# Every batch's ninth chunk moved to the last four tiles, and router weights and row fills issued one at a time between the loads

## The chip, the core and the metric

The kernel runs on one core of one Trainium2 chip. The metric is the device time of one execution in microseconds (us); lower is better. The times below are the median of three executions, and the profile is of one further execution of the same program.

## What is computed

Attention inside chunks of 64 tokens, then a two-level mixture of experts on the result, all in float32:

```python
B, H, S, D = 8, 8, 576, 64                 # 9 chunks of 64 tokens in each batch
scores = (q_c @ k_c.T) / 8                 # within one chunk of 64, per head
out = softmax(scores) @ v_c
x = out.transpose(0, 2, 1, 3).reshape(4608, 512)   # one row per token
g_idx = argmax(x @ w_group)                # 4 groups
e_idx = argmax(x @ w_expert[g_idx])        # 4 experts in each group
h = relu(x @ w1[g, e])                     # 512 -> 1024
y = combined_weight * (h @ w2[g, e])       # 1024 -> 512, written to the token's row
```

Each token goes to one of 16 experts. The order in which tokens are worked on is free, as long as each result lands in its own row.

## The kernel before

**Tiles.** The 72 chunks are numbered c = 0..71 and two neighbours make a tile of 128 tokens, so there are 36 tiles. Before, chunk c is chunk c % 9 of batch c // 9. `load_qk(n)`, written Qn, brings q and k of four chunks (two tiles) into one buffer, two tokens in a partition, so that four chunks fill 128 partitions and one chunk fills 32. `load_v(t)`, written Vt, brings v of one tile, 64 partitions for a chunk. Both ask `spans(c0, n)` into which pieces a run of chunks falls, and issue one DMA for each piece; a piece ends where a batch ends. The q and k buffers are three in rotation, those of v eight. All these DMAs are issued by SyncE (SP) on one queue, one behind the other.

**The loop.** Iteration t of the first stage (t = 0..26; then a hand-written string, TAIL) issues for TensorE: the scores of tile t (`stage_b`, line 308), P times V of tile t-2 (`stage_pv`, line 344), two `stage_a` steps that transpose raw q and k of tiles further on (line 286; step a(4n) is the first to read load Qn), the transpose of the probabilities (331) and of x (373). After every fourth tile a group of 512 tokens is routed: `stage_e1` multiplies x by the router weights `wg` (line 380), first in iteration 7; `stage_e3` and `place` compute each token's row in its expert's region of the DRAM buffer `xs`, and GpSimd (POOL) writes the rows there by four indirect DMAs (line 514). The order of TensorE, VectorE and ScalarE is the program's own; that of SP and POOL is made by a scheduler from the program's order and what each step waits for.

**What else SP issues.** After the two steps of an iteration come the load Q(t/2+4) in even iterations, V(t+4), and what `EXTRA[t]` lists: `Z0`..`Z4` (`prefill`) fill five blocks of 128 rows of `xs` from the tile `pad`, and `G0` (`load_wg`) brings the router weights, five DMAs in a row, and makes two small copies on VectorE and one on GpSimd. The indirect writes to `xs` wait until all five fills have landed.

**The second stage** works expert by expert on the rows of `xs`, from line 738 on. How many units it has, and of which kinds, follows from how many tokens each expert has in all; the expert that goes first is the one with most tokens after four groups.

Of the kernel before, what the change touches and what calls it, by code (L numbers as in the profile page):

```python
# [19 lines left out]
P = 128  # L20
B, H, SEQ, HD = 8, 8, 576, 64
CH = 64
NCH = SEQ // CH
N = B * SEQ
D = H * HD
F = 1024
G, EG = 4, 4
E = G * EG
NT = N // P
NG = 4  # L30
RPE = N // P
GL = NT // NG - 1
# [10 lines left out]

HEAD = "Q0 @ Q1 V0 Q2 V1 V2 V3 a0 a1"
FIRST = "a2 a3 Q3 a4 a5 a6"
EXTRA = {0: "Z0 Z1", 1: "G0 Z2", 2: "Z3", 3: "Z4",
         24: "F0", 26: "F1"}
T0 = 27
TAIL = ("m2 a60 b27 E0 p25 V31 s27 15 l5 n25 c26 m1 P0 a61 e27 j0 x24 25 b28 F2 m1 F3 s28 P1 a62 c27 p26 m1 e28 a63 V32"
# [8 lines left out]
C_ID, C_TRI, C_SEL, C_BASE, C_IOTA4, C_TID, C_T17, C_I64, C_J128, C_FORCE, C_BE, C_PBASE, C_E, C_PM, C_I16, C_PJ, C_PQ, C_PMIN, C_PNEED, C_N = (  # L58
    0, 128, 256, 276, 292, 296, 332, 349, 413, 449, 450, 451, 452, 453, 455, 471, 473, 475, 476, 477)
# [4 lines left out]
BIG = 1 << 20  # L64


def constants():
    c = np.zeros((P, C_N), np.float32)
    p = np.arange(P)
    c[:, C_ID:C_ID + P] = np.eye(P)  # L70
    c[:, C_TRI:C_TRI + P] = p[:, None] < p[None, :]
    for j in range(20):
        c[p % 32 == j, C_SEL + j] = 1.0
    for j, rows in enumerate((32, RE - 32)):
        c[j, C_BASE:C_BASE + E] = np.arange(E) * rows * P
    c[:, C_IOTA4:C_IOTA4 + 4] = np.arange(4)
    c[:, C_TID:C_TID + NT] = np.arange(NT)[None, :] * P + p[:, None]

    o = np.roll(np.arange(E1), -1)
    c[:E1, C_T17:C_T17 + E1] = o[:, None] < o[None, :]  # L80
    c[:E1, C_I64:C_I64 + 64] = np.arange(64)
    c[:E1, C_J128:C_J128 + RPE] = np.arange(RPE) * P
    c[:E1, C_FORCE] = o < FORCED
    c[:E, C_BE] = (np.arange(E) * RE - E * RE) * P
    c[:E, C_PBASE] = np.arange(E) * RE * P
    c[0, C_PMIN] = c[0, C_PNEED] = 2 * P
    c[1:FORCED - 1, C_PNEED] = P
    c[:E1, C_E] = np.arange(E1)
    c[0, C_PM], c[0, C_PM + 1] = 1.0, -1.0
    c[:, C_I16:C_I16 + E] = np.arange(E) - 64.0  # L90
    for j in range(2):
        c[0, C_PJ + j] = j * P + P - 1
        c[0, C_PQ + j] = j * P + 64 * RE * P - E * RE * P
    return c


def moe_kernel(tc, q, k, v, w_group, w_expert, w1, w2, cst, out):
    nc = tc.nc
    w1 = w1.rearrange("g e d f -> (g e) d f")
    w2 = w2.rearrange("g e f d -> (g e) f d")  # L100
    with ExitStack() as ctx:
# [12 lines left out]
        nc.gpsimd.memset(pad, 0.0)  # L114
        nc.gpsimd.memset(pad[:, D:D + 1].bitcast(I32), N)

# [94 lines left out]
        with ExitStack() as c1:  # L211
# [15 lines left out]
            wg = cpool.tile([P, 4, 32], F32, name="wg")  # L227
# [9 lines left out]
            def spans(c0, n):  # L237
                out, c = [], c0
                while c < c0 + n:
                    b, j = divmod(c, NCH)  # L240
                    m = min(c0 + n - c, NCH - j)
                    out.append((c - c0, m, b, j))
                    c += m
                return out

            def load_qk(n):

                if n == 0:
                    raw = lpool.tile([P, 2, 2, H, HD], F32, name="qk", tag="big")
                    parts = [(1, t, raw[:, t], slice(None)) for t in range(2)]  # L250
                else:
                    raw = lpool.tile([P, 2, H, 2 * HD], F32, name="qk", tag="big")
                    parts = [(2, 2 * n, raw, slice(None))]
                st["q", n] = raw
                for A, t0, dst, hs in parts:
                    R = CH // A
                    for x, src in enumerate((q, k)):
                        for i, m, b, j in spans(2 * t0, 2 * A):
                            nc.sync.dma_start(  # L259
                                dst[i * R:(i + m) * R, x, hs],  # L260
                                src[b, hs, j * CH:(j + m) * CH, :].rearrange("h (r a) d -> r h (a d)", a=A))

            def load_v(t):

                va = vbufs[t % NV]
                for i, m, b, j in spans(2 * t, 2):
                    nc.sync.dma_start(va[i * CH:(i + m) * CH, :, 0:HD], v[b, :, j * CH:(j + m) * CH, :].rearrange("h s d -> s h d"))
                st[t] = dict(va=va)
# [339 lines left out]
                    while routing and next(routing[0], True):  # L608
                        routing.pop(0)

            def load_wg(_):
                nc.vector.tensor_copy(tri, cs[:, C_TRI:C_TRI + P])
                nc.vector.tensor_copy(base, cs[0:2, C_BASE:C_BASE + E])
                nc.gpsimd.tensor_copy(identr, ident)
                nc.sync.dma_start(wg[:, :, 0:G], w_group.rearrange("(c p) g -> p c g", p=P))
                for g in range(G):
                    nc.sync.dma_start(wg[:, :, 4 + 4 * g:8 + 4 * g], w_expert[g].rearrange("(c p) e -> p c e", p=P))

            def last(t):
                return t >= 0 and t % NG == NG - 1  # L620
# [8 lines left out]
            def run(seq):  # L629
                g = dict(P=prep_hi, j=prep_lo, J=lambda i: prep_lo(i, nc.vector), X=first_x, U=first_xl, E=exponent, L=first_l1, H=first_hi, D=first_lo, W=prep2_hi, w=prep2_lo, y=lambda i: prep2_lo(i, nc.vector), F=first_loads, R=reload, V=load_v,  # L630
                         Q=load_qk, G=load_wg, Z=prefill, a=stage_a)
                f = dict(b=stage_b, s=stage_sub, c=stage_ct, e=stage_exp, p=stage_pv, n=stage_norm, x=stage_xt)
                for z in seq.split():
                    if z[0] == "m":
                        more(int(z[1:]))
                    elif z[0] in g:
                        g[z[0]](int(z[1:]))
                    elif z[0] == "1":
                        stage_e1(int(z[1:]))
                    elif z[0] == "l":  # L640
                        stage_lts(int(z[1:]))
                    elif z[0] == "2":
                        stage_e2(int(z[1:]))
                    elif z[0] == "3":
                        stage_e3(int(z[1:]))
                    elif 0 <= int(z[1:]) < NT:
                        f[z[0]](int(z[1:]))

            with tc.manual_schedule(engines={mybir.EngineType.PE, mybir.EngineType.DVE, mybir.EngineType.Activation}):
# [4 lines left out]
                for t in range(T0):  # L654
# [13 lines left out]
                    if last(t - 4):  # L668
                        run("2%d" % ((t - 4) // NG))
                    run(EXTRA.get(t, ""))  # L670
                run(TAIL)
# [33 lines left out]
        py = [ps.tile([P, 512], F32, name="py%d" % j) for j in range(2)]  # L705
        names = "Z M A In Ga Gb XT XEa XEd L1 R T Ha Hd L2 Y Sc Is Pb Pc Pd X Se V TP TV TB P1a P1d P2a P2d X4 N".split()
        names += ["r1%d" % j for j in range(NP)] + ["r2%d" % j for j in range(NP)]
# [30 lines left out]
        with tc.tile_critical(no_gpsimd_drain=True):  # L738
            with nc.Block(no_gpsimd_drain=True) as blk:
# [355 lines left out]
                def _(ve):  # L1095
                    def W(n, x):
                        ve.wait_ge(S[n], x)
# [43 lines left out]
                    def total(u, b):  # L1141
# [4 lines left out]
                        else:  # L1146
                            for x in range(2):
                                m = ve.tensor_tensor(out=to[:, x], in0=ph[b + x][:, 0:256], in1=to[:, x], op=ALU.add)
                        m.then_inc(S["N"], 1)
                        W("Ha", 4 * u + (b + 1))  # L1150
                        W("N", 4 * u + (b - 3))
                        return to
# [335 lines left out]
```

## Time and profile before

| | |
|---|---|
| median of 3 executions | 670.1 us (667.87, 670.1, 671.76) |
| the profiled execution | 668.08 us |
| its span, first to last instruction | 666.4 us |
| TensorE, mean granted clock | 0.988 of full speed |
| first stage, with the routing | about the first 215 us |

The profile has a page with busy times and the costliest groups, and views of the trace: the waits in total, the timeline of one engine, the busy time and DMA traffic of chosen windows, and the chain of work that ended last. In a timeline, what stands in brackets is the time an engine was idle before the row and what ended it. PE is TensorE, DVE VectorE, ACT ScalarE, POOL GpSimd; SPq is the queue of SyncE, whose rows are the issues of DMAs and not the transfers.

### The profile page before, as it was taken

The numbers are of one execution on the slowest core, as the hardware profiler recorded it, in microseconds if no ns is written. First come the engines' busy times: TensorE is split into PE (matmuls) and PEld (weight loads), VectorE is DVE, ScalarE is ACT, GpSimd is POOL, SyncE is SP. The second block draws the span as 40 slices with busy tenths as digits, with TensorE's granted clock in tenths as the row PEclk, the third lists the DMA queues.
The fourth block names the chain that finished last, engine by engine and source line by source line (L and its number), as shares of the span: only waits on it lengthen the run. The fifth ranks groups of instructions, "written<-read, shape, count | busy, mean of one in ns | idle before, by whom it ended". The sixth has DMA issues, their size and how long they took to land.

```text
span 666.4 us, 16268 instructions
## 1 busy us (share of the span) xinstructions
PE 628.3 (94%) x5423; PEld 531.3 (80%) x5424; DVE 433.2 (65%) x800; ACT 354.2 (53%) x534; POOL 172.2 (26%) x255
## 2 busy tenths in 40 slices
PE   5999888989789899999999999999999999999996
PEld 4887776876668778888888888888888888888884
DVE  3657755876577668851577886674663888977331
ACT  3676766876575255731357565362531756644211
POOL 1002022124332333211134523232212233313220
PEclk9899899998999899999999999999999999999999
DMA  9999978799615488751084966727261368761100
GB/s 210 228 202 238 265 203 213 169 296 256 204 65 176 142 293 328 270 194 63 25 300 179 350 246 227 251 104 251 90 233 56 135 243 315 276 234 57 38 32 31
DMA packets 116333, 128.02 MB, mean 192 GB/s; under 512 B 48894, under 2 KB 83966, under 8 KB 116288
## 3 DMA queue, kind: packets, MB, share of 16 engines
q1 hardware_dynamic: 105424, 93.76, 48.6%
q0 software_dynamic: 10864, 33.64, 14.2%
q8 instruction: 30, 0.49, 0.3%
q14 instruction: 15, 0.12, 0.1%
HBM read 106.23 MB, written 21.93 MB: 192 GB/s over the span
## 4 chain that ended last, share of the span: by engine, by line
PE 78%; DMA 6%; DVE 6%; issue 3%; SPq 2%; ACT 2%; POOL 1%; another core or an unknown queue 0%; POOLq 0%; DVEq 0%; ACTq 0%
PE py L870 27%; PE ph L856 14%; PE pxt L856 5%; PE ph L839 5%; PE sc L308 4%; PE o L344 4%; PE tp L286 3%; PE lgk L856 3%; DMA qk<-in_k_dram 2%; PE lgk L380 2%; PE tp L331 2%; PE pxt L755 2%; PE ph L801 2%; SPq L259 1%; PE tp L373 1%
## 5 line engine op out<-in xcount | busy, mean ns | idle before, releaser
L1395 POOL DMA_INDIRECT out_dram<-xl,io x37 | 41.8, 1130 | 148.9 <-DVE xl L1104 130.3
L856 PE MATMUL ph<-xt,w1h 128*128 128x512 f32 x280 | 76.3, 394 | 0.9 <-issue 0.5
L1118 DVE TENSOR_TENSOR w2l<-w2r,w2h 128x1024 fp32r<-128x1024 f32 x60 | 69.4, 1217 | 2.8 <-ACT w2h L1059 2.0
L1041 ACT ACTIVATE hth<-ph 128x512 fp32r<-128x512 f32 x28 | 16.8, 599 | 102.2 <-PE ph L856 96.3
L1114 DVE TENSOR_TENSOR w1l<-w1r,w1h 128x2048 fp32r<-128x2048 f32 x28 | 64.0, 2293 | 8.8 <-ACT w1h L1017 7.8
L870 PE MATMUL py<-w2h,hth 128*128 128x512 f32 x264 | 67.8, 399 | 0.0
L870 PE MATMUL py<-w2l,hth 128*128 128x512 f32 x264 | 65.4, 390 | 0.0
L870 PE MATMUL py<-w2h,htl 128*128 128x512 f32 x264 | 65.2, 389 | 0.0
L289 ACT COPY qT<-tp 64x512 f32<-64x512 f32 x68 | 42.5, 624 | 35.7 <-PE tp L286 25.6
L870 PEld LDWEIGHTS py<-w2l,hth 128*128 128x128 f32 x264 | 49.6, 188 | 10.7
L870 PEld LDWEIGHTS py<-w2h,htl 128*128 128x128 f32 x264 | 49.6, 188 | 10.3
L1017 ACT CAST w1h<-w1r 128x2048 fp32r<-128x2048 f32 x28 | 53.4, 1911 | 4.9 <-DMA w1r<-in_moe_w_dram 2.9
L870 PEld LDWEIGHTS py<-w2h,hth 128*128 128x128 f32 x264 | 47.6, 188 | 10.2 <-ACT hth L1089 0.9
L856 PEld LDWEIGHTS ph<-xt,w1h 128*128 128x128 f32 x280 | 48.9, 189 | 8.6 <-issue 0.7
L1021 ACT CAST w2h<-w2r 128x2048 fp32r<-128x2048 f32 x28 | 52.7, 1933 | 1.1 <-DMA w2r<-in_moe_w_dram 1.0
L514 POOL DMA_INDIRECT xs<-x,pos x24 | 24.4, 1016 | 102.2 <-DMA va<-in_v_dram 52.0
L344 PE MATMUL o<-va,pT 64*64 64x65 f32 x1152 | 44.1, 223 | 5.6 <-issue 2.8
L308 PEld LDWEIGHTS sc<-kT,qT 64*64 64x64 f32 x1152 | 39.1, 140 | 11.6 <-issue 10.0
L308 PE MATMUL sc<-kT,qT 64*64 64x64 f32 x1152 | 44.6, 227 | 4.0 <-issue 2.7
L1104 DVE TENSOR_SCALAR xl<-py,io 128x512 f32<-128x512 f32 x33 | 24.5, 747 | 36.3 <-PE py L870 36.2
L286 PE MATMUL tp<-cs,qk 128*128 128x128 f32 x272 | 43.4, 284 | 4.8 <-DMA qk<-in_q_dram 2.3
L856 PEld LDWEIGHTS ph<-xt,w1l 128*128 128x128 f32 x280 | 43.0, 188 | 6.1 <-DVE w1l L1114 0.3
(282 smaller groups left out, 1225.6 us busy)
## 6 DMA issues: line engine op xcount, KB each, us to landing
w1r<-in_moe_w_dram SPq DMA_DIRECT2D x30, 1024.0 KB, 4.8
w2r<-in_moe_w_dram SPq DMA_DIRECT2D x30, 1024.0 KB
xgr<-xs POOLq DMA_DIRECT2D x38, 257.0 KB, 3.3
va<-in_v_dram SPq DMA_DIRECT2D x32, 256.0 KB
qk<-in_q_dram SPq DMA_DIRECT2D x11, 512.0 KB
qk<-in_k_dram SPq DMA_DIRECT2D x11, 512.0 KB
w1r<-in_moe_w_dram POOLq DMA_DIRECT2D x2, 1024.0 KB
w2r<-in_moe_w_dram POOLq DMA_DIRECT2D x2, 1024.0 KB
```

The source lines that it names most:

```text
L286: nc.tensor.transpose(pt[:, hp, :], st["q", n // 4][:, z, 2 * hp + x], ident)
L289: y = [(nc.vector.tensor_copy if z and not a else nc.scalar.copy)(to[:, a], pt[64 * a:64 * a + 64]) for a in range(2)]
L308: nc.tensor.matmul(sc[HALF[x], hp, c], lhsT=st["T", u, 0][HALF[x], hp, k0:k0 + CH], rhs=st["T", u, 1][HALF[x], hp, k0:k0 + CH], start=True ...
L344: nc.tensor.matmul(o[HALF[c], x, hp * W:hp * W + W], lhsT=pT[HALF[c], hp, HALF[x]], rhs=s["va"][HALF[c], 2 * hp + x], start=True, stop=True)
L839: m = pe.matmul(ph[n], a_[:, c, 0:P], w_[:, c, n * 512:(n + 1) * 512], start=(i == 0), stop=(i == 11))
L856: m = pe.matmul(o if i < 4 else o[:, 0:256], (w1l if i > 3 else w1h)[:, c, f * P:(f + 1) * P], both[:, c] if i < 4 else xth()[:, c, :], st ...
L870: m = pe.matmul(py[j], a_[:, f, half[j]], w_(b, f), start=(i == 0), stop=(i == 23))
L1017: lambda b, s, j: ac.copy(wt[b][0][:, s], w1r[j]), K1, js)
L1021: lambda b, s, j: ac.copy(wt[b][2 + j], w2r[j]), K2)
L1114: lambda b, s, j: ve.tensor_sub(wt[b][1][:, s], w1r[j], wt[b][0][:, s].bitcast(F32)), K1, js)
L1118: m = ve.tensor_sub(wt[b][4 + 2 * j + i], w2r[j][:, 2 * i:2 * i + 2], wt[b][2 + j][:, 2 * i:2 * i + 2].bitcast(F32))
L1395: gp.indirect_dma_start(out, bass.IndirectOffsetOnAxis(ap=io[:, j, 0:1].bitcast(I32), axis=0), yb[:, j, :], None, bounds_check=N - 1, oob_ ...
```

## The change

`chunk(c)` gives the batch and the place of chunk c. The first 64 chunks are chunks 0 to 7 of each batch in turn; the last eight are the ninth chunks of batches 0 to 7. So tiles 0..31 and loads Q0..Q15 lie within a batch, and tiles 32..35 and loads Q16 and Q17 take each chunk from another batch. The table of token numbers in `constants()` follows the new order. `load_wg(i)` issues one of the five router DMAs, and `EXTRA` spreads these over iterations 0 to 3 and the five fills over iterations 2 to 7.

```diff
+EVEN = NCH - 1
-EXTRA = {0: "Z0 Z1", 1: "G0 Z2", 2: "Z3", 3: "Z4",
+EXTRA = {0: "G0 G1", 1: "G2", 2: "G3 Z0", 3: "G4", 4: "Z1", 5: "Z2", 6: "Z3", 7: "Z4",
          24: "F0", 26: "F1"}
+def chunk(c):
+    return divmod(c, EVEN) if c < B * EVEN else (c - B * EVEN, EVEN)
-    c[:, C_TID:C_TID + NT] = np.arange(NT)[None, :] * P + p[:, None]
+    for n in range(B * NCH):
+        b, j = chunk(n)
+        c[n % 2 * CH:n % 2 * CH + CH, C_TID + n // 2] = b * SEQ + j * CH + np.arange(CH)
@@ spans
-                    b, j = divmod(c, NCH)
-                    m = min(c0 + n - c, NCH - j)
+                    b, j = chunk(c)
+                    m = min(c0 + n - c, EVEN - j) if j < EVEN else 1
@@
-            def load_wg(_):
+            def load_wg(i):
+                if i:
+                    nc.sync.dma_start(wg[:, :, 4 * i:4 * i + 4], w_expert[i - 1].rearrange("(c p) e -> p c e", p=P))
+                    return
                 nc.vector.tensor_copy(tri, cs[:, C_TRI:C_TRI + P])
                 nc.vector.tensor_copy(base, cs[0:2, C_BASE:C_BASE + E])
                 nc.gpsimd.tensor_copy(identr, ident)
                 nc.sync.dma_start(wg[:, :, 0:G], w_group.rearrange("(c p) g -> p c g", p=P))
-                for g in range(G):
-                    nc.sync.dma_start(wg[:, :, 4 + 4 * g:8 + 4 * g], w_expert[g].rearrange("(c p) e -> p c e", p=P))
```

The instructions of TensorE, ScalarE and GpSimd stand in the same order as before; VectorE makes its two copies one iteration earlier. What moves is SP's row of DMA issues. Load Q2 on SP, at the start, with V0 and V1 around it, before:

```order
L267 DMA va_126<-in_v_dram 128x8x64
L259 DMA qk<-in_q_dram 32x8x128
L259 DMA qk<-in_q_dram 96x8x128
L259 DMA qk<-in_k_dram 32x8x128
L259 DMA qk<-in_k_dram 96x8x128
L267 DMA va_128<-in_v_dram 128x8x64
```

and after:

```order
L274 DMA va_126<-in_v_dram 128x8x64
L266 DMA qk<-in_q_dram 128x8x128
L266 DMA qk<-in_k_dram 128x8x128
L274 DMA va_128<-in_v_dram 128x8x64
```

Four issues became two; Q4, Q6, Q11, Q13 and Q15 were cut in the same way before and are whole now.

SP from load Q4 to V7, in which Q5 is the second pair of qk rows, before:

```order
L259 DMA qk<-in_q_dram 64x8x128 x2
L259 DMA qk<-in_k_dram 64x8x128 x2
L267 DMA va_134<-in_v_dram 64x8x64 x2
L624 DMA xs<-pad 128x514 x2
L267 DMA va_136<-in_v_dram 128x8x64
L615 DMA wg<-in_moe_w_group_dram 128x4x4
L617 DMA wg<-in_moe_w_expert_dram 128x4x4 x4
L624 DMA xs<-pad 128x514
L259 DMA qk<-in_q_dram 128x8x128
L259 DMA qk<-in_k_dram 128x8x128
L267 DMA va_138<-in_v_dram 128x8x64
L624 DMA xs<-pad 128x514
```

and after:

```order
L274 DMA va_134<-in_v_dram 128x8x64
L625 DMA wg<-in_moe_w_group_dram 128x4x4
L620 DMA wg<-in_moe_w_expert_dram 128x4x4
L274 DMA va_136<-in_v_dram 128x8x64
L620 DMA wg<-in_moe_w_expert_dram 128x4x4
L266 DMA qk<-in_q_dram 128x8x128
L266 DMA qk<-in_k_dram 128x8x128
L274 DMA va_138<-in_v_dram 128x8x64
L620 DMA wg<-in_moe_w_expert_dram 128x4x4
L632 DMA xs<-pad 128x514
L274 DMA va_140<-in_v_dram 128x8x64
L620 DMA wg<-in_moe_w_expert_dram 128x4x4
```

Three fills and two router DMAs that stood ahead of Q5 now stand behind it; the last router DMA stands behind V7.

SP at the end of the loop, from load Q16 on, in which the tiles va_134, va_136, va_138, va_140 and va_126 hold V28 to V32, before:

```order
L259 DMA qk<-in_q_dram 128x8x128
L259 DMA qk<-in_k_dram 128x8x128
L267 DMA va_134<-in_v_dram 128x8x64
L267 DMA va_136<-in_v_dram 128x8x64
L259 DMA qk<-in_q_dram 128x8x128
L259 DMA qk<-in_k_dram 128x8x128
L267 DMA va_138<-in_v_dram 128x8x64
```

and after:

```order
L274 DMA va_136<-in_v_dram 128x8x64
L274 DMA va_138<-in_v_dram 128x8x64
L266 DMA qk<-in_q_dram 32x8x128 x4
L266 DMA qk<-in_k_dram 32x8x128 x4
L266 DMA qk<-in_q_dram 32x8x128 x4
L266 DMA qk<-in_k_dram 32x8x128 x4
L274 DMA va_140<-in_v_dram 128x8x64
L274 DMA va_126<-in_v_dram 64x8x64 x2
```

Q16 and Q17 are eight issues of 32 partitions each and stand next to each other; V28 to V30 stand ahead of them, and the last four V loads are two issues of 64 partitions each. From V18 on the V loads stand up to three places earlier among the Q loads than before.

## Rows read from the trace of the kernel before

**Rows 1.** The page, busy us (share of the span) x instructions.

```profile
PE 628.3 (94%) x5423; PEld 531.3 (80%) x5424; DVE 433.2 (65%) x800; ACT 354.2 (53%) x534; POOL 172.2 (26%) x255
```

**Rows 2.** Waits of PE in 0 to 210 us: us in total, times, longest.

```profile
PE tp L286 <- DMA qk<-in_q_dram: 2.3, 2, 1.5
...
PE tp L286 <- DMA qk<-in_k_dram: 1.8, 2, 1.4
```

**Rows 3.** Timeline of PE, iteration 1: start us, us, what [idle before <-releaser].

```profile
16.65 0.63 PE L286 MATMUL tp<-cs,qk 128*128 128x128 f32 x4 [1.48 <-DMA qk<-in_q_dram]
...
19.14 0.96 PE L286 MATMUL tp<-cs,qk 128*128 128x128 f32 x4 [1.42 <-DMA qk<-in_k_dram]
```

**Rows 4.** Timeline of PE, iteration 7 and the start of iteration 8.

```profile
40.93 1.15 PE L308 MATMUL sc<-kT,qT 64*64 64x64 f32 x32
...
43.85 0.63 PE L286 MATMUL tp<-cs,qk 128*128 128x128 f32 x4 [0.84 <-DMA qk<-in_q_dram]
44.41 1.07 PE L380 MATMUL lgk<-xT,wg 128*32 128x512 f32 x8
...
47.85 1.15 PE L308 MATMUL sc<-kT,qT 64*64 64x64 f32 x32
```

**Rows 5.** Timeline of PE, iteration 23, which has the steps of iteration 7.

```profile
127.35 1.15 PE L308 MATMUL sc<-kT,qT 64*64 64x64 f32 x32
...
129.95 1.06 PE L380 MATMUL lgk<-xT,wg 128*32 128x512 f32 x8
...
132.84 0.86 PE L308 MATMUL sc<-kT,qT 64*64 64x64 f32 x22
```

**Rows 6.** Windows: us, busy by engine, then PEclk, DMA share, GB/s.

```profile
20.00:25.00 5.00, 5.00 (x87) 4.74 (x88) 3.43 (x9) 1.67 (x3) 0.00 (x0) 0.73 0.93 229
25.00:30.00 5.00, 4.94 (x116) 4.60 (x114) 3.54 (x7) 4.22 (x8) 0.00 (x0) 1.00 1.21 220
...
34.00:38.00 4.00, 4.00 (x90) 3.76 (x88) 2.94 (x6) 3.35 (x6) 0.00 (x0) 1.00 0.81 82
```

**Rows 7.** Timeline of SP, its DMA issues: start us, us, what.

```profile
28.86 2.55 SPq L624 DMA_DIRECT2D xs<-pad  x2
...
31.98 1.02 SPq L615 DMA_DIRECT2D wg<-in_moe_w_group_dram  x1
...
37.26 0.38 SPq L259 DMA_DIRECT2D qk<-in_q_dram  x1
...
43.52 0.43 SPq L267 DMA_DIRECT2D va<-in_v_dram  x1
...
57.03 1.72 SPq L267 DMA_DIRECT2D va<-in_v_dram  x1
```

**Rows 8.** The chain that ended last, 0 to 100 us: start us, us, what.

```profile
37.68 8.60 DMA qk<-in_k_dram
```

**Rows 9.** The page, DMA issues: KB each, median us from issue to landing.

```profile
w1r<-in_moe_w_dram SPq DMA_DIRECT2D x30, 1024.0 KB, 4.8
```

**Rows 10.** Timelines of POOL and PE: scatters of groups 0 and 3, tiles 11, 14, 26.

```profile
61.36 1.12 POOL L514 DMA_INDIRECT xs<-x,pos  x1 [52.03 <-DMA va<-in_v_dram]
...
130.15 0.99 POOL L514 DMA_INDIRECT xs<-x,pos  x1 [11.83 <-DVE pr L319]
...
60.45 1.15 PE L308 MATMUL sc<-kT,qT 64*64 64x64 f32 x32
...
79.12 1.09 PE L308 MATMUL sc<-kT,qT 64*64 64x64 f32 x30
...
143.10 1.11 PE L308 MATMUL sc<-kT,qT 64*64 64x64 f32 x31
```

**Rows 11.** Timelines of SP (parts of Q11, k of Q17) and PE (first use of Q17).

```profile
83.02 1.07 SPq L259 DMA_DIRECT2D qk<-in_q_dram  x2
...
150.00 0.99 SPq L259 DMA_DIRECT2D qk<-in_k_dram  x1
...
171.65 0.66 PE L286 MATMUL tp<-cs,qk 128*128 128x128 f32 x4
```

## The prediction

> **What bounds the kernel now.** I read the page first. TensorE is busy 94% of the span [rows 1], so the question is only where it waits, and whether the change reaches such a wait. The change touches the loads of the first stage, so the second view is PE's waits there. PE waited for a load of q or k in the steady loop four times in all, twice for q (2.3 us, longest 1.5) and twice for k (1.8 us, longest 1.4) [rows 2]. Two of these four are in iteration 1, for load Q2 [rows 3], and two in iteration 7, for load Q5: 0.84 us for q, and for k the 0.4 us that is left of the 1.8 [rows 2, 4]. No other wait of PE is for a load that this change moves, so whatever it gives must come through these two places, or through the order of events behind them.
>
> The third view is the windows. From 20 to 30 us the DMA engines are busy (share 0.93 and 1.21) and move 220 to 229 GB/s; from 34 to 38 they move only 82 GB/s [rows 6]. SP's timeline says what was in the queue then: two fills at 28.86, the five router DMAs from 31.98 on, and only at 37.26 load Q5 [rows 7]. The chain that ended last goes through that place: k of Q5, issued at 37.68, landed 8.60 us later [rows 8]. So around 31 to 46 us the DMA queue, and the order in it, sets PE's pace; elsewhere PE sets its own.
>
> **Part 1: Q2, Q4 and Q6 whole.** Same bytes, two issues fewer each. The window that holds mainly the cut Q4 moved 220 GB/s, the one with the whole Q3 229 [rows 6]. Q2 is 2 x 512 KB, 1.05 MB: 4.77 us at the one rate and 4.58 at the other, 0.2 us. That is the low bound. The high bound is that the two saved issues count in full: an issue without a backlog takes 0.53 us (1.07 for two) [rows 11], so 0.2 + 1.07 = 1.3 us. Since the DMA engines are at a share around 1 there, issues are mostly hidden by the backlog, and I take a value near the low bound, 0.4 us. PE waits 1.42 us for k of Q2 [rows 3], so all of it reaches PE. Of Q4 and Q6, on which PE did not wait, the saving lies ahead of Q5 and of the last fill and is used below.
>
> The rows show whole loads 4% faster than cut ones. The Trainium skill (SBUF — State Buffer, Door 1: The DMA port swizzle) says that a transfer to 32 or 64 partitions reaches half of SBUF's ports, with 189 to 196 GB/s against 328 for 128 partitions at 1 MiB. By that rule Q2 would take 5.35 us cut and 3.2 whole, a term of 2.1 us in place of 0.2; the trace does not agree in size (229 against 220), and this result is a rival below. The same rule speaks against the other end of the change, where Q16 and Q17 come in pieces of 32 partitions.
>
> **Part 2: fills and router DMAs moved behind Q5.** How long would iteration 7 be with no late load? Iteration 23 has the same steps (scores, P times V, the router product) and no wait for a load: from 127.35 to 132.84, 5.49 us [rows 5]. Iteration 7 took 47.85 - 40.93 = 6.92 us [rows 4]. The difference, 1.43 us, is what late loads cost there, and the term if Q5 comes early enough. It does: three fills, of 1.27 us each (2.55 for two) [rows 7], and two router DMAs leave the queue ahead of it. That alone is 3.8 us, more than the two waits.
>
> What is late next is the last router DMA. It stood ahead of Q5 and now stands behind V7, while the router product of iteration 7 needs all five. When is it issued? V7 was issued at 43.52 and done issuing at 43.95 [rows 7]. Ahead of that place stand three fills fewer (3.8 us), Q2 and Q4 whole (0.8 us), and the router DMAs, which cost (1 - 82/225) x 4 = 2.5 us of moved bytes when they stood in a row [rows 6]; between loads I let half of that go, 1.3 us. So it is issued at about 38.0. Landing: 4.8 us is the median of the weight loads [rows 9], 8.60 the late k [rows 8]; so 42.8 to 46.6, and I take 42.8, since the router DMA is small. When is it wanted? Iteration 7 starts 0.4 us earlier, at 40.5, and the router product comes 2.60 us after its start (129.95 - 127.35) [rows 5]: 43.1. So it lands just in time. At the late bound it is 3.5 us late, and the term is 1.43 - 3.5 = -2.1 us. I take +1.4 us, because the nearer row for a small DMA is the lower one.
>
> VectorE's two small copies come one iteration earlier, in a place where it waits for PE; nothing.
>
> **Part 3: the fills come later.** The scatter of the first group waits for the last fill. The last fill stands where V11 stood, issued at 57.03 [rows 7]; with 1.2 us for Q2, Q4 and Q6 and 1.3 us for the router DMAs off, 54.5, and with 4.8 to 8.60 us to land, 59.3 to 63.1. The scatter started at 61.36, 0.91 us after tile 11's scores at 60.45 [rows 10]; with the 1.8 us of parts 1 and 2 it would be ready at 59.5. So it is held up by 0 to 3.6 us. Does that cost? Nothing on PE waits for the scatter itself; behind it on POOL is only the token-number copy of group 3, three iterations later. But the stretch in which a group is scattered is slow: tiles 11 to 14 took 79.12 - 60.45 = 18.67 us. In group 3 the scatter started later against the tiles, 2.80 us after tile 23's scores, and tiles 23 to 26 took 143.10 - 127.35 = 15.75 us [rows 5, 10]. If the delay brings the first group into that position, up to 2.9 us come back. The other end is a small loss; I put it at -0.5 us, as much as the place between 0.91 and 2.80 could shift either way. One case is little, so I take a quarter of it, 0.7 us.
>
> **Part 4: Q16, Q17 and the last V loads in pieces.** Twelve more issues for q and k, at most 12 x 0.53 = 6.4 us of SP [rows 11]. Q17's k was issued at 150.00; with the longest landing in the rows, 8.60, it is there by 158.6, and PE first needs Q17 at 171.65 [rows 8, 11]. That is 13 us of cover, so it costs nothing; Q16 has more. If the cover were gone, the price would be up to 6.4 us.
>
> The rule of the Trainium skill named above gives 5.5 us for 1.05 MB in pieces of 32 partitions instead of 3.2, 2.3 us more for each of the two loads, which this cover also hides.
>
> **The second stage** is the same: each expert has the same tokens in all. I assume the same expert goes first.
>
> **The sum.** 0.4 + 1.4 + 0.7 + 0 = 2.5 us. Behind these places the loads have cover (part 4), and what is left, PE's own steps and the scatters that they release, moves up together. The profiled execution took 668.08 us: 665.6. It lies 2.0 us under the median of 670.1, so against the median the forecast is 667.6 us, 0.37% faster. A measurement of this kernel can tell about 0.5%, 3.35 us, from no change.
>
> **Rivals.**
> (a) The last router DMA is late: PE waits at the router product instead of at Q5. For it: the order is tight, 42.8 against 43.1. Against: the queue ahead is shorter by some 6 us. It is a loss from the point where it lands more than 1.4 + 0.4 us late, after 44.9; at the far bound, 46.6, it costs 2.1 - 0.4 = 1.7 us, 671.8 us, slower than before. Part 3 left out.
> (b) The first scatter falls as in group 3 and Q2's gain is larger: 1.43 + 2.9 + 0.4 to 1.3, 4.7 to 5.6 us, 664.5 to 665.4. For it: the one late scatter in the trace had the short stretch. Against: one case.
> (c) Whole loads are so much faster than cut ones that both waits for Q2 go (1.48 + 1.42) [rows 3], and with them the stretch at half clock behind them: 20 to 25 us ran at a granted clock of 0.73 [rows 6], a loss of 1.35 us. With part 2: 5.7 us, 664.4. Against: 229 against 220 GB/s [rows 6]. The Trainium skill's rule on ports (SBUF — State Buffer, Door 1) is what speaks for it.
> (d) The change does not reach the end: something later, such as the weights of the first expert, sets the time again. Then 670.1. Against: in the view of PE's waits in the first stage, no wait is for a DMA of weights; the late ones for loads are those of q and k [rows 2].
>
> **Chances.** Forecast, 1 to 3.3 us faster: 0.53. (a) 0.13, (b) 0.20, (c) 0.06, (d) 0.08. The range takes in (b), (c) and (d) and stops within (a): 664.0 to 670.8. Faster by over 0.5%: (b), (c) and a little of the forecast with the spread of a median, 0.31. Slower by over 0.5% needs a router DMA at 48 us or later, beyond the bound, or an unknown cost: 0.06. Within 0.5%: 0.63.
>
> **What would show it.** In the profile of after: no wait of PE for q or k in iteration 7, and iteration 7 near 5.5 us (part 2); a wait before the router product for `wg` is rival (a). The waits for Q2 down by 0.4 us (part 1) or gone (c). POOL's first scatter started by a landed fill, with tiles 11 to 14 at 16 to 18 us (part 3) or unchanged. No wait of PE for q, k or v after 140 us (part 4). The prediction is wrong if tile 14 starts at the same time as before, or if the gain of the first 80 us is given back later.

## The result, and the profile of the changed kernel

The changed kernel takes 663.5 us (median of 6, 661.82 to 664.74) where the kernel before takes 670.24 us on the same chip: a ratio of 0.9907, 95% interval 0.9884 to 0.9929, so 6.7 us or 0.93% faster. The forecast was 667.6 us in 664.0 to 670.8. The direction is right and the place in the code is right; the time lies 0.5 us under the low end and 1.0 us under the region of rival (b) (664.5 to 665.4), and a gain of more than 0.5% had been given a chance of 0.31 only. The profiled execution took 663.07 us, its span is 661.2 us, 5.2 us less than before.

PE's busy time is what it was [rows 1], since its instructions are the same. The page of the changed kernel:

```profile
PE 628.6 (95%) x5423; PEld 531.9 (80%) x5424; DVE 433.2 (66%) x800; ACT 354.0 (54%) x534; POOL 169.7 (26%) x255
```

**Load Q2.** PE's waits in 0 to 60 us (us in total, times, longest) now hold one wait for a load in the steady loop, of 0.6 us, where there were four with 4.1 us in all [rows 2]:

```profile
PE tp L288 <- DMA qk<-in_q_dram: 5.1, 1, 5.1
PE tp L293 <- DMA qk<-in_k_dram: 0.6, 1, 0.6
```

PE's timeline shows both waits of iteration 1 [rows 3] gone: tile 2's scores start at 17.95 us in place of 20.03. What is late next is k of load Q3, in iteration 3:

```profile
17.39 0.63 PE L293 MATMUL tp<-cs,qk 128*128 128x128 f32 x4
17.95 1.15 PE L315 MATMUL sc<-kT,qT 64*64 64x64 f32 x32
...
25.65 0.63 PE L293 MATMUL tp<-cs,qk 128*128 128x128 f32 x4 [0.56 <-DMA qk<-in_k_dram]
```

In the chain that ended last (start us, us, what) it stands as the transfer that took the longest to land in the first 100 us:

```profile
18.14 7.37 DMA qk<-in_k_dram
```

The windows in which Q2 and behind it V1 to V3 move (us, busy by engine, PEclk, DMA share, GB/s), first of the kernel before, then of the changed one, show that more bytes moved in the same time:

```profile
12.00:18.00 6.00, 4.24 (x57) 3.64 (x55) 3.45 (x5) 4.91 (x9) 0.00 (x0) 1.00 1.25 215
```

```profile
12.00:18.00 6.00, 5.66 (x62) 4.72 (x61) 3.74 (x7) 5.00 (x9) 0.00 (x0) 1.00 1.25 261
```

215 GB/s with Q2 in four pieces, 261 with it in two. And the window that the prediction had taken for a whole load's, 20 to 25 us at 229 GB/s [rows 6], moves 286 now (262 in the second profile of the changed kernel, `e9_after_again` below):

```profile
20.00:25.00 5.00, 4.94 (x96) 4.37 (x90) 4.14 (x10) 3.60 (x7) 0.00 (x0) 1.00 1.11 286
```

**Iteration 7.** Load Q5 is issued at 30.07 us, where it was 37.26 [rows 7], and nothing is waited for. The iteration takes 43.86 - 38.37 = 5.49 us, where it was 6.92 [rows 4], exactly as long as iteration 23 was [rows 5]. The last router DMA is issued at 36.26 and is there when the router product starts (PE, then SP's issues of Q5's q, of the last router DMA and of the last fill):

```profile
38.37 1.15 PE L315 MATMUL sc<-kT,qT 64*64 64x64 f32 x32
...
40.97 1.06 PE L387 MATMUL lgk<-xT,wg 128*32 128x512 f32 x8
...
43.86 1.15 PE L315 MATMUL sc<-kT,qT 64*64 64x64 f32 x32
```

```profile
30.07 0.45 SPq L266 DMA_DIRECT2D qk<-in_q_dram  x1
...
36.26 0.93 SPq L620 DMA_DIRECT2D wg<-in_moe_w_expert_dram  x1
...
51.26 1.41 SPq L632 DMA_DIRECT2D xs<-pad  x1
```

**The first scatter.** VectorE had the rows of the first group ready at 56.46 us, as tile 11's scores began; POOL's first indirect DMA started at 58.40, 1.94 us after those scores where it was 0.91 [rows 10]. It had waited for the last fill, issued at 51.26. (For this wait the profile names an instruction of VectorE; that it was the fill is read across the profiles. In the eight of fourteen in which the scatter came more than 1 us after its rows were ready, it started 6.55 to 7.67 us after the issue of the last fill, while the time from the ready rows was anything from 1.1 to 4.5 us. In the four in which the last fill was issued 15 us or more ahead, it started 0.9 us after the rows.) Tiles 11 to 14 took 71.41 - 56.46 = 14.95 us, where they took 18.67 [rows 10] (PE and POOL of the changed kernel):

```profile
56.46 1.15 PE L315 MATMUL sc<-kT,qT 64*64 64x64 f32 x32
58.40 1.12 POOL L521 DMA_INDIRECT xs<-x,pos  x1 [49.13 <-DVE m L323]
62.48 1.21 PE L315 MATMUL sc<-kT,qT 64*64 64x64 f32 x28
...
71.41 1.15 PE L315 MATMUL sc<-kT,qT 64*64 64x64 f32 x32
```

**What is given back.** Tile 14 starts 79.12 - 71.41 = 7.7 us earlier, but the span ends only 5.2 us earlier. The kernel before ran at a granted clock of 0.5, that is at 1.2 GHz, in two stretches of that time (about 19 to 23 us, behind the waits for Q2, and 70 to 74 us, behind the first scatter):

```profile
20.00:22.00 2.00, 2.00 (x37) 1.97 (x38) 0.90 (x3) 0.62 (x1) 0.00 (x0) 0.50 0.87 156
...
72.00:74.00 2.00, 2.00 (x23) 1.88 (x21) 1.97 (x10) 0.05 (x1) 0.19 (x1) 0.53 1.12 288
```

The changed kernel has neither, but has two later ones that the kernel before has not, at or behind a tile in which PE also stood still (tiles 15 and 24), and there tiles 16 and 24 take 1.5 us longer than in the kernel before:

```profile
86.00:88.00 2.00, 2.00 (x42) 2.00 (x42) 1.09 (x2) 0.78 (x2) 0.00 (x0) 0.50 1.11 215
...
130.00:132.00 2.00, 2.00 (x22) 1.88 (x18) 1.97 (x7) 0.20 (x1) 0.00 (x0) 0.50 0.86 154
```

By starts of tiles the gain is thus: 2.1 us at tile 2 and 2.6 at tile 7 from the loads ahead, 1.4 in iteration 7, 3.7 in tiles 11 to 14, and 2.3 to 2.5 lost again behind tile 15.

### The profile page after: what moved, and what is told of

The parts are those of the page before. It is cut to its first block, busy times and chain, and to the rows that moved or that the text cites. A ratio compares the mean times of both kernels' runs of the same rounds, so it can differ in the third digit from the quotient of the medians.

```text
span 661.2 us, 16283 instructions
## 1 busy us (share of the span) xinstructions
PE 628.6 (95%) x5423; PEld 531.9 (80%) x5424; DVE 433.2 (66%) x800; ACT 354.0 (54%) x534; POOL 169.7 (26%) x255
## 4 chain that ended last, share of the span: by engine, by line
PE 79%; DMA 6%; DVE 5%; issue 4%; ACT 3%; POOL 1%; another core or an unknown queue 0%; DVEq 0%; POOLq 0%; SPq 0%; ACTq 0%
PE py L878 27%; PE ph L864 13%; PE pxt L864 5%; PE sc L315 5%; PE ph L847 5%; PE o L351 4%; PE tp L293 4%; PE lgk L864 3%; PE tp L338 2%; PE lgk L387 2%; DMA w1r<-in_moe_w_dram 2%; PE ph L809 2%; PE tp L380 2%; PE pxt L763 2%; DMA xs<-x,pos 1%
## 5 line engine op out<-in xcount | busy, mean ns | idle before, releaser
L351 PEld LDWEIGHTS o<-va,pT 64*64 64x64 f32 x1152 | 39.0, 137 | 9.5 <-issue 5.2
```

The costliest lines, as they stand in the source:

```text
L351: nc.tensor.matmul(o[HALF[c], x, hp * W:hp * W + W], lhsT=pT[HALF[c], hp, HALF[x]], rhs=s["va"][HALF[c], 2 * hp + x], start=True, stop=True)
```

## The experiments

Twelve further runs were timed on three chips: `e1` to `e4` on chip A, `e5` and `e7` to `e9` on chip B, `e6` and `e10` to `e12` on chip C. Every ratio is to the kernel before on the same chip. There the kernel before takes 653.45 us on chip A, 670.54 on B and 655.12 on C, against 670.24 on the chip on which the changed kernel was first timed. The chips differ by 2.6%, more than the change does, so total times of different chips are not compared here. Each run has one profile.

### Each half of the change alone

`e1_order_only` has the new order of chunks, so Q2, Q4 and Q6 whole, with fills and router DMAs where they were:

```diff
-EXTRA = {0: "G0 G1", 1: "G2", 2: "G3 Z0", 3: "G4", 4: "Z1", 5: "Z2", 6: "Z3", 7: "Z4",
+EXTRA = {0: "Z0 Z1", 1: "G0 Z2", 2: "Z3", 3: "Z4",
```

> The new chunk order alone: loads whole until Q15, router weights and fills issued as before (five router DMAs in a row and three fills ahead of Q5). Theory P (a load into 32, 64 or 96 partitions moves its bytes slower than one into 128): both waits of PE for Q2 (1.5 and 1.4 us) are gone as in the changed kernel, tile 2 starts near 18 us in place of 20, the wait for Q5 in iteration 7 stays at 0.5 to 2 us, and the time is 2 to 4 us under before, 666 to 668. Theory O (only the order behind Q5 matters): Q2's waits stay near 1.2 us each and the time is within 1 us of before, 669 to 671.

`e2_issue_only` has the old order and the new places of fills and router DMAs:

```diff
-                    b, j = chunk(c)
-                    m = min(c0 + n - c, EVEN - j) if j < EVEN else 1
+                    b, j = divmod(c, NCH)
+                    m = min(c0 + n - c, NCH - j)
```

> The old chunk order with the new places of router DMAs and fills. Theory P: Q2 stays cut, so the waits of 1.5 and 1.4 us for it stay and tile 2 starts at 20.0 us; iteration 7 takes 5.5 us in place of 6.9, and with the scatter held up by the last fill tiles 11 to 14 take 15 to 16.5 us in place of 18.7; gain 3 to 4.5 us, 665.5 to 667. If the two parts do not add up, because each hides the other's wait, the gains of this run and of the order alone together are under 5 us or over 8 us, where both at once gave 6.7.

Measured: 646.32 us, ratio 0.9899 (0.9866 to 0.9931), for the order alone; 652.05 us, 0.9966 (0.9935 to 0.9996), for the issues alone. PE's timeline of the first has no wait for Q2 and both for Q5, 1.08 and 1.48 us:

```profile
17.93 1.15 PE L315 MATMUL sc<-kT,qT 64*64 64x64 f32 x32
...
41.62 0.63 PE L293 MATMUL tp<-cs,qk 128*128 128x128 f32 x4 [1.08 <-DMA qk<-in_q_dram]
45.31 0.63 PE L293 MATMUL tp<-cs,qk 128*128 128x128 f32 x4 [1.48 <-DMA qk<-in_k_dram]
46.74 1.15 PE L315 MATMUL sc<-kT,qT 64*64 64x64 f32 x32
```

That of the second has both for Q2, a third behind them of 2.78 us for k of Q3, and none in iteration 7 (43.49 to 48.98, 5.5 us):

```profile
16.63 0.63 PE L286 MATMUL tp<-cs,qk 128*128 128x128 f32 x4 [0.96 <-DMA qk<-in_q_dram]
19.06 0.63 PE L286 MATMUL tp<-cs,qk 128*128 128x128 f32 x4 [1.37 <-DMA qk<-in_k_dram]
19.62 1.15 PE L308 MATMUL sc<-kT,qT 64*64 64x64 f32 x32
...
29.24 0.63 PE L286 MATMUL tp<-cs,qk 128*128 128x128 f32 x4 [2.78 <-DMA qk<-in_k_dram]
...
43.49 1.15 PE L308 MATMUL sc<-kT,qT 64*64 64x64 f32 x32
```

So each half takes away the waits that Parts 1 and 2 put down to it, and leaves the others. The order is the larger half, where the prediction had put 0.4 of its 2.5 us; both sizes missed the expectations (7.1 us gained where 2 to 4 were expected, and 1.4 where 3 to 4.5 were). At tile 7 the order alone is 43.49 - 38.46 = 5.0 us ahead of the issues alone: 1.7 us at tile 2, 2.0 more at tile 4 by the wait for Q3, and the rest in a stretch at half clock behind that wait (30 to 34 us). The two gains together, 1.01% and 0.34%, are 1.35% or 8.5 us, over the 8 us that the expectation had set as the sign that the halves do not add up. The changed kernel itself was not run on chip A, so this stays open; `e3_q2_by_partitions` and `e4_q2_by_heads` below, which have both halves but for Q2, gain 1.1% there.

### Why a whole load is faster: pieces or partitions

Both kernels are the changed one with Q2 alone in four issues again. `e3_q2_by_partitions` cuts it as it was cut, into 32 and 96 partitions:

```diff
+                        if n == 2:
+                            _, _, b, j = pieces[0]
+                            pieces = [(0, 1, b, j), (1, 3, b, j + 1)]
```

> The changed kernel with load Q2 alone cut again, q and k each into pieces of 32 and 96 partitions, 4 issues in place of 2. Theory P (partitions): from 12 to 18 us the DMA engines move 205 to 225 GB/s in place of 234 to 289, PE waits 2 to 3 us for Q2, tile 2 starts 1.5 to 2.5 us later than in the changed kernel, and the time is 1 to 3 us above it, 664.5 to 666.5. Theory I (issues): the same loss, since the issues are four.

`e4_q2_by_heads` cuts it into 2 and 6 heads, so that every piece still fills 128 partitions:

```diff
+                            for hh in ((slice(0, 2), slice(2, 8)) if n == 2 else (hs,)):
```

> The changed kernel with load Q2 cut into as many pieces of the same sizes, but by heads: 2 and 6 heads into all 128 partitions, 4 issues in place of 2. Theory P (partitions): no loss, 250 to 290 GB/s from 12 to 16 us, tile 2 near 18 us, time as the changed kernel, 662.5 to 664.5. Theory I (issues): the loss of the run cut by partitions, tile 2 near 20 us.

Measured: 645.41 us, 0.9886 (0.9838 to 0.9933), and 645.88 us, 0.9891 (0.9855 to 0.9928); the totals don't tell them from each other or from `e1_order_only`. PE's timeline shows the waits, and SP's the issues of Q2's k. First the cut by partitions, then the cut by heads:

```profile
11.34 1.59 SPq L270 DMA_DIRECT2D qk<-in_k_dram  x2
...
18.89 0.63 PE L297 MATMUL tp<-cs,qk 128*128 128x128 f32 x4 [1.24 <-DMA qk<-in_k_dram]
...
44.75 1.86 PE L391 MATMUL lgk<-xT,wg 128*32 128x512 f32 x8 [2.52 <-DMA wg<-in_moe_w_expert_dram]
```

```profile
12.66 1.49 SPq L267 DMA_DIRECT2D qk<-in_k_dram  x2
...
19.19 0.55 PE L294 MATMUL tp<-cs,qk 128*128 128x128 f32 x3 [1.22 <-DMA qk<-in_k_dram]
...
44.98 1.06 PE L388 MATMUL lgk<-xT,wg 128*32 128x512 f32 x8 [1.90 <-DMA wg<-in_moe_w_expert_dram]
```

From the issue of Q2's q (8.76 and 9.31 us on SP) to the end of the wait for its k it took 10.13 us cut by partitions and 9.88 cut by heads; in the other profiles of the cut load 10.15 to 11.10 (four), in those of the whole load in which PE waited 8.55 to 9.39 (five). So by this measure four issues cost about 1 to 1.6 us, cut by heads as well as by partitions. Two other readings of the same profiles don't agree with that. From the issue of Q2's k to the end of the wait it took 6.53 us cut by heads (19.19 - 12.66), as in the whole load (6.66 to 7.42), and 7.55 to 8.33 in the five profiles cut by partitions; the time that the cut by heads lost lies ahead of that, in the issue of q, 3.31 us on SP against 2.33 to 2.72 cut by partitions. And from 14 to 18 us it moved 244 GB/s, between the 217 to 227 of the cuts by partitions and the 255 to 272 of the whole load. With one profile of the cut by heads, how much of the loss comes from the number of issues and how much from the partitions stays open.

The second thing here was not sought: Q2 being slow again pushes the whole queue back, and the last router DMA is late, by 2.52 and 1.90 us at the router product of iteration 7, which takes 9.72 and 7.46 us. That is rival (a).

### The place of the first scatter

Theory S: where the scatter stands against the tiles sets how long tiles 11 to 14 take, early (0.9 us after tile 11's scores) being the dear place. Rival C: that length belongs to the chip or the execution. For them the two kernels ran once more, and with them `e5_before_late_scatter`, the kernel before with the first scatter one step of the loop later,

```diff
             def place(g):
                 V = nc.vector
+                if g == 0:
+                    yield
```

and `e7_fills_earlier`, the changed kernel with its fills earlier, so that they don't hold up the scatter:

```diff
-EXTRA = {0: "G0 G1", 1: "G2", 2: "G3 Z0", 3: "G4", 4: "Z1", 5: "Z2", 6: "Z3", 7: "Z4",
+EXTRA = {0: "G0 G1", 1: "G2", 2: "G3 Z0", 3: "G4 Z1", 4: "Z2", 5: "Z3", 6: "Z4",
```

> The kernel before once more, unchanged, profiled on the chip on which the kernels sent with it run, so that starts of tiles can be laid side by side. Both theories: tile 2 starts near 20.0 us, iteration 7 takes 6.9 us, the first scatter starts 0.9 us after the scores of tile 11. Theory S (the place of the first scatter against the tiles sets how long tiles 11 to 14 take): tile 11 to tile 14 again 18 to 19 us, as in the first profile (18.67). Rival C (that length belongs to the chip or the execution): another number, 13.5 to 15 us, with the scatter in the same place.

> The changed kernel once more, unchanged, on the same chip as the others of this call. Ratio to before 0.990 again (0.985 to 0.994) if the gain is of the kernel and not of the first chip. Tile 2 starts at 17.9 us (2.1 earlier than before), iteration 7 takes 5.5 us, the first scatter is held up by the last fill and starts near 1.9 us after the scores of tile 11. Theory S: tiles 11 to 14 take 15 us. Rival C: 13.5 to 15 us here, and the same in the kernel before on this chip.

> The kernel before with one thing changed: the first group's scatter is issued one step of the loop later, everything else in place. Theory S: the scatter starts 4 to 6 us after the scores of tile 11 in place of 0.9, tiles 11 to 14 take 15 to 16.5 us in place of 18.7, and the kernel is 2 to 3.5 us faster than before (ratio 0.995 to 0.997). Rival C: tiles 11 to 14 take the same as in the kernel before on this chip, and the time is the same (0.998 to 1.002).

> The changed kernel with the fills Z1 to Z4 one iteration earlier, so that the last has landed before the first scatter could start: the scatter starts about 0.8 us after the scores of tile 11, as in the kernel before, in place of 1.9. Theory S: tiles 11 to 14 take 17 to 18.7 us again and the kernel loses 2 to 3.5 us against the changed kernel (ratio to before 0.993 to 0.996). Rival C: tiles 11 to 14 as in the changed kernel on this chip, ratio 0.990 as there. Load Q5 may have one fill more ahead of it: a wait of up to 0.8 us in iteration 7 in both.

Measured, with the start of the first indirect DMA after the start of tile 11's scores, and the length of tiles 11 to 14:

| kernel | us | ratio (95%) | scatter after | tiles 11 to 14 | half clock in them |
|---|---|---|---|---|---|
| before, first profile | 670.24 | | 0.91 | 18.67 | yes |
| `e8_before_again` | 670.74 | 1.0002 (0.9967 to 1.0038) | 0.46 | 17.74 | yes |
| `e7_fills_earlier` | 667.67 | 0.9964 (0.9935 to 0.9994) | 0.90 | 18.60 | yes |
| `e5_before_late_scatter` | 669.13 | 0.9995 (0.9971 to 1.0019) | 2.91 | 17.41 | yes |
| after, first profile | 663.5 | 0.9907 (0.9884 to 0.9929) | 1.94 | 14.95 | no |
| `e9_after_again` | 662.8 | 0.9897 (0.9858 to 0.9936) | 3.03 | 15.68 | no |

The gain holds on chip B. Taking the delay by the fills away (`e7_fills_earlier`) brings the long stretch back, 18.60 us in place of 15.68, which speaks for the delay as a part of the gain. The rows of that kernel, PE and POOL:

```profile
44.17 1.93 PE L387 MATMUL lgk<-xT,wg 128*32 128x512 f32 x8 [3.02 <-DMA xs<-pad]
...
61.25 1.15 PE L315 MATMUL sc<-kT,qT 64*64 64x64 f32 x32
62.15 1.12 POOL L521 DMA_INDIRECT xs<-x,pos  x1 [52.85 <-DMA qk<-in_q_dram]
70.46 1.20 PE L315 MATMUL sc<-kT,qT 64*64 64x64 f32 x32
```

It loses 4.9 us against the changed kernel, and these rows hold both places: the router product waits 3.02 us (0.79 us in `e9_after_again`), and tile 11 takes 9.2 us. The first is again rival (a): the edit puts one fill more right behind the last router DMA, which was issued at 38.16 us (37.98 in `e9_after_again`) and took SP 2.46 us to issue (0.78 there). Why, the profile doesn't say; it puts the wait down to a fill.

But a late scatter alone is not enough. In `e5_before_late_scatter` it came as late as in `e9_after_again`, and the stall only moved from tile 11 (5.5 us now) to tile 12 (8.0 us), with a stretch at half clock behind it; the 2 to 3.5 us that theory S expected did not come:

```profile
61.50 1.15 PE L308 MATMUL sc<-kT,qT 64*64 64x64 f32 x32
64.41 1.12 POOL L516 DMA_INDIRECT xs<-x,pos  x1 [55.17 <-DVE rc L354]
66.99 1.14 PE L308 MATMUL sc<-kT,qT 64*64 64x64 f32 x31
...
75.00 1.15 PE L308 MATMUL sc<-kT,qT 64*64 64x64 f32 x32
```

So S holds in the changed order and fails in the old one. What differs is whether the half clock follows: in `e8_before_again` the granted clock from 66 to 72 us was 0.88, 0.50 and 0.76 in windows of 2 us, a loss of (0.12 + 0.50 + 0.24) x 2 = 1.7 us, of the 2.1 us by which its tiles 11 to 14 are longer than those of `e9_after_again`. Why the clock falls in the one and not in the other stays open.

And on chips A and C tile 11 has no such stall, nor has tile 19, and tile 15 has 0.6 us of it in one profile of eight. `e1_order_only`, PE and POOL, with the scatter 0.91 us after tile 11's scores as in [rows 10], and tile 11 at 5.5 us:

```profile
59.35 1.15 PE L315 MATMUL sc<-kT,qT 64*64 64x64 f32 x32
60.26 1.12 POOL L521 DMA_INDIRECT xs<-x,pos  x1 [50.96 <-DMA va<-in_v_dram]
...
64.84 1.15 PE L315 MATMUL sc<-kT,qT 64*64 64x64 f32 x32
```

That is rival C's point: the same instructions in the same place come with 3.7 us on one chip and with nothing on another. What the profiles of chips A and C have in its place is a stall in tile 18, which takes 5.1 to 8.9 us where it takes 4.2 to 4.6 on the slower chips. It comes ahead of the third scatter, with no indirect DMA running, and the profile shows nothing that PE waited for ("issue"). In `e2_issue_only`, whose third scatter starts at 101.29 us:

```profile
97.53 1.15 PE L344 MATMUL o<-va,pT 64*64 64x65 f32 x32 [2.87 <-issue]
```

So a stall of this kind can come without a scatter, and that the scatter causes the other is argued from their places only. These stalls may be most of what the chips differ by: tile 35 starts at 185.0 us in `e2_issue_only`, which gains 2.2 us there, and at 198.8 in `e8_before_again`. Part 3's gain was seen only where the kernel before takes 670 us.

### Attempts to gain more

`e6_late_scatters` moves the scatters of groups 0 to 2 one step later; `e10_routers_earlier` brings the last two router DMAs one iteration earlier; `e11_both` does both; `e12_split_scatters` puts the second half of each of these scatters one step later.

```diff
             def place(g):
                 V = nc.vector
+                if g < 3:
+                    yield
```

```diff
-EXTRA = {0: "G0 G1", 1: "G2", 2: "G3 Z0", 3: "G4", 4: "Z1",
+EXTRA = {0: "G0 G1", 1: "G2 G3", 2: "G4 Z0", 4: "Z1",
```

```diff
+                h = 2 if g < 3 else NG
+                for k in range(0, NG, h):
+                    if k:
+                        yield
                     with nc.allow_low_precision(reason="a sum of one whole number and zeros"):
-                        V.tensor_reduce(out=pos, in_=ps, axis=AX.X, op=ALU.add)
+                        V.tensor_reduce(out=pos[:, k:k + h], in_=ps[:, k:k + h], axis=AX.X, op=ALU.add)
```

> The changed kernel with the scatters of groups 0 to 2 one step of the loop later (the row computation and the four indirect DMAs with it). Theory S (a scatter 2 to 3 us after its tile's scores stalls the engines 1.5 to 2.5 us, one 0.9 us after them 3.7 to 4.2): the long tiles 15 and 19 (9.2 us where 5.5 is the length without a stall) lose 1.3 to 2.2 us each, so 2.6 to 4.4 us off the changed kernel, ratio to before 0.983 to 0.987. Rival M (the stall goes along with the scatter at the same price): tiles 16 and 20 are longer by what 15 and 19 are shorter, ratio 0.990 as in the changed kernel.

> The changed kernel with the third and fourth router DMA one iteration earlier, so that the last stands ahead of V6 and no longer behind V7 and the fill Z0. Theory (the last router DMA lands just in time in the changed kernel, which waited 0.8 us for it in one execution and 0 in another): issued near 34 to 35 us in place of 36.3 and 38.0, no wait for wg in iteration 7, which takes 5.5 us; load Q5 has one small DMA more ahead of it and still is not waited for. Gain over the changed kernel 0 to 0.8 us, ratio 0.989 to 0.990. Rival: the router DMA ahead of Q5 makes PE wait for Q5 instead, iteration 7 at 6 us or more.

> Both edits, the scatters of groups 0 to 2 one step later and the last router DMA ahead of V6. Theory S: the two gains add, 2.6 to 5.2 us off the changed kernel, ratio to before 0.982 to 0.987. Rival M: only the router part is left, 0.989 to 0.990.

> The changed kernel with the scatters of groups 0 to 2 in two halves: the rows of two tiles and their two indirect DMAs in the old place, the other two one step later (one more VectorE instruction of 0.2 us for each group). Theory B (the stall comes from four indirect DMAs back to back): half as long or none, tiles 15 and 19 at 5.5 to 7.3 us in place of 9.2, the next tile at most 1 us longer, 2 to 6 us off, ratio 0.981 to 0.987. Theory S expects half of that, since the first half still starts 0.9 us after the scores. Rival M: the same sum of stalls in smaller pieces, ratio 0.990.

Measured: 646.2, 646.24, 646.64 and 646.02 us; ratios 0.9873 (0.9834 to 0.9911), 0.9881 (0.9833 to 0.993), 0.9872 (0.9825 to 0.992) and 0.9879 (0.9839 to 0.992). The four can't be told apart, nor from the 0.990 of the changed kernel. Chip C was one without the stall (tile 11 took 5.5 us in all four), so theories S, M and B of the expectations are not told apart either; these runs are inconclusive on scatters. On the router DMA they say a little: issued at 34.81 us it was not waited for (`e10_routers_earlier`), issued at 37.79 it was, for 1.04 us (`e6_late_scatters`), and 36.91 was in time (`e12_split_scatters`). In `e11_both`, issued at 35.67, PE stood 1.01 us in the same place without a releaser in the profile; so "earlier" was not shown to be safe. Where the gain of about 8 us comes from on such a chip was not traced, since the kernel before was not profiled there.

## Why the prediction was right, and where it was not

**What bounds the kernel: right.** In the first profile of the changed kernel the gain came at Q2, Q5 and the first scatter, and at no other wait that the profile shows.

**Part 1: mechanism right, size wrong.** The term was 0.4 us (bounds 0.2 to 1.3); measured are 2.1 us at tile 2 on the first chip, and 1.7 us by the mean start of tile 2 over all profiles (20.03 us in the six with Q2 cut, 18.34 in the eight with it whole). Two steps of the prediction failed. The rate: "the window that holds mainly the cut Q4 moved 220 GB/s, the one with the whole Q3 229". Q4's pieces were issued at 21.91 and 24.02 us, inside the window of 20 to 25 us that was taken for Q3's, so both windows held cut loads, and their small difference said nothing about whole ones (215 against 261 where Q2 itself moves). SP of the kernel before:

```profile
21.91 2.07 SPq L259 DMA_DIRECT2D qk<-in_q_dram  x2
24.02 2.29 SPq L259 DMA_DIRECT2D qk<-in_k_dram  x2
```

And the choice: the low bound was taken because the DMA engines were busy and would hide two issues; the high bound, 1.3 us, was nearer. Rival (c) stated the outcome (both waits gone, and the half clock behind them) with a chance of 0.06. Its reason is borne out in direction at most: by the Trainium skill (SBUF — State Buffer, Door 1: The DMA port swizzle) pieces of 32 or 64 partitions move at 189 to 196 GB/s against 328. Here it was 215 against 261; and the prediction had put the lower rate to all of Q2, of which three quarters are pieces of 96 partitions. What the number of issues and what the partitions cost is open, as said above.

**Part 2: right in the first profile, with nothing to spare.** 1.43 us forecast and 6.92 - 5.49 = 1.43 measured. The router DMA was to be issued near 38.0, to land at 42.8 and to be wanted at 43.1; it was issued at 36.26 and wanted at 40.97 in one execution, without a wait, and issued at 37.98, there at 42.47, 0.79 us late, in `e9_after_again`. There iteration 7 took 6.35 us against the 6.47 of `e8_before_again`, 0.1 us of the 1.4. Of the four profiles with this queue two have the full term (5.49 us, and 5.52 in `e12_split_scatters`) and two have not (6.35, and 6.61 in `e6_late_scatters`), so that it came out whole the first time is partly luck:

```profile
37.98 0.78 SPq L620 DMA_DIRECT2D wg<-in_moe_w_expert_dram  x1
```

```profile
42.47 1.06 PE L387 MATMUL lgk<-xT,wg 128*32 128x512 f32 x8 [0.79 <-DMA wg<-in_moe_w_expert_dram]
```

"Just in time" was the right reading, and rival (a) is real: it came at 1.9 to 3.0 us in the three kernels with more issues in that part of the queue, and at 1.04 us in `e6_late_scatters`, which has the queue of the changed kernel. `e1_order_only` and `e2_issue_only` show the term by its presence and its absence.

**Part 3: the hold-up right, the gain behind it larger and not explained.** The last fill did hold up the scatter, by 1.94 - 0.91 = 1.0 us, inside the 0 to 3.6 us given. Of "up to 2.9 us" a quarter was taken, 0.7; measured are 3.7 us on the first chip and 2.1 on chip B. The step that failed is the bound: 2.9 came from one case and left out that a stretch at half clock, 1.6 us of the kernel before's 18.67 (tile 12 took 5.47 us, tile 13 with the same steps 3.91), could go as well; on chip B it is 1.7 of the 2.1. That the place of the scatter alone would bring the gain is not borne out (`e5_before_late_scatter`).

**Part 4: right for the changed kernel where it was profiled, not on chips A and C.** Behind 140 us PE waits for no load of q, k or v in either profile of it. But on the faster chips the tiles come earlier, and in two of the seven profiles of the new order there PE waits for Q16, which is now in pieces: 1.67 us for its q in `e1_order_only` (last piece issued by 136.13 us), 1.28 us for its k in `e10_routers_earlier`. "Q16 has more" cover failed there.

```profile
147.27 0.63 PE L293 MATMUL tp<-cs,qk 128*128 128x128 f32 x4 [1.67 <-DMA qk<-in_q_dram]
```

**The sum.** 2.5 us were forecast. With the measured terms, 2.1 + 1.4 + 3.7 = 7.2 us at tile 14 (7.7 by its starts); "what is left moves up together" failed by 2.3 to 2.5 us, since two stretches at half clock came back later. The errors of Parts 1 and 3 are of one sign, and the give-back took half of them off; that the time lies only 0.5 us outside the range is luck.

## What to carry to other kernels

Before a window's rate is put down to one transfer, read the issues in the DMA queue's timeline: it must hold nothing of the other kind. When a load that is waited for leaves the queue earlier, look at the next one, and at what stands last in the queue that somebody needs (here the last router DMA, in time when it was issued at 36.26 or 36.91 us and late when at 37.79 or 37.98); and give terms that remove a wait of PE at least the chance that the half clock behind the wait goes with it, and comes back elsewhere.

## What was not expected of the hardware

While the same scatter runs, four indirect DMAs from POOL, tile 11 is 3.7 us longer where the kernel before takes 670 us, and not on the two chips where it takes 653 to 655. In the kernel before, ScalarE and VectorE stand idle from about 63 to 67 us, behind PE's transposes that ended at 63.2 us by the trace; they go on 0.9 us after POOL's last indirect DMA (65.36 + 0.97 us):

```profile
65.36 0.97 POOL L514 DMA_INDIRECT xs<-x,pos  x1 [0.30 <-issue]
...
67.21 0.17 DVE L352 TENSOR_SCALAR rc<-o 128x8 f32<-128x8 f32 x1 [3.83 <-PE tp L286]
67.26 1.23 ACT L289 COPY qT<-tp 64x512 f32<-64x512 f32 x2 [4.67 <-PE tp L286]
```

The profile names no cause for it, and the stall was not taken apart further. The granted clock falls to 0.5 for 3 to 4 us behind many stalls of PE, but not behind all (none follows the wait of 1.48 us for Q5 in `e1_order_only`): the first 215 us have one to five such stretches in the six profiles on the slower chips, in places that change from execution to execution, at about 1.5 us each.
